# A joint inverse of two units by 16-row corners, with the middle block by matrix products, in a fused delta-rule attention and feed-forward kernel

## The chip, the cores and the metric

The kernel runs on one core of a Trainium2 chip. The metric is device time in microseconds (us) of one launch, as the median of several runs; before the change three runs gave a median of 634.74 us (633.33 to 635.35). The engines of the core are named PE (TensorE, matrix products; its weight load is listed as PEld), DVE (VectorE), ACT (ScalarE), POOL (GpSimd) and SP (SyncE, whose queue issues nearly all DMAs). Each engine takes its instructions in program order.

## The reference

Two layers follow each other, in float32: a linear attention with the delta rule over 4 batches, 8 heads, 768 tokens and head size 48, and a feed-forward layer with squared ReLU on 3072 tokens of width 384.

```
k_n = k / (norm(k) + 1e-6)
for t in range(S):
    y[t]  = q[t] @ state
    v_old = state^T @ k_n[t]
    state = state + beta[t] * outer(k_n[t], v[t] - v_old)
x   = y as (tokens, heads * 48)
out = relu(x @ w_in) ** 2 @ w_out          # w_in 384 x 2048, w_out 2048 x 384
```

## The kernel before

**Units.** The sequence is cut into 12 units of 64 tokens (`C`), each for all 4 batches and 8 heads, which gives 32 blocks of 64 by 64. In such a block the recurrence becomes the inverse of a lower triangle, built from beta and the products of the keys. The block is inverted by 32-row halves (`HB`): the two diagonal blocks of 32 rows by elimination on DVE, the block between them by two matrix products (`whole`). `solved` multiplies V by the inverse T, `onward` moves the state on and gives the attention's output `y`, and `moe` runs the feed-forward layer on a unit's 256 tokens. From unit 1 on, a list of places (`weave`) mixes the parts of one unit's attention into the matrix products of another unit's `moe`.

**The start.** Units 0 and 1 are treated together ahead of that. `load` and `normalize` fetch and normalize the keys, `static` forms the products of keys with keys and then of queries with keys, and sends the 32-row blocks through DRAM (`to_blocks`, L375) into one tile `lt` with 128 rows (L382), a row of which is one of the 32-by-32 triangles of units 0 and 1. `invert` with `both` set then inverts all 128 at once: 31 steps of two DVE instructions each (L453 multiplies a column by a row, L456 subtracts), between two scalings by beta (L446, L458). L464 transposes the result into `dd`. From `dd`, DMAs carry the diagonal blocks to their places in the T tiles `tt0` and `tt1` (L479) and a copy for the product with the upper block to `t1t` (L475), which L517 transposes for unit 0. L510 and L522 are the two products of `whole`, L512 and L528 the copies that follow them.

**The weights.** All 28 pieces of the feed-forward weights stay on chip, each split into a high and a low part. A piece goes through five stations: `fetch` (L126, DMA), `scaled` (L140, ACT), `words` (L148, L150, L152, DVE, into staging tiles `a` or `r` and `rest` or `h_l`), `high` (L158, ACT) and `low` (L165, L166 on PE, L167 on ACT). The staging tiles `a` and `r` have two buffers each, so the words of the third piece of a kind need the low of the first to have read them. Twenty pieces are split ahead of the first `moe` step, eight of them ahead of the inverse; the calls of `early` set how many stand between the parts of unit 0's chain. Before a low is issued, up to three highs may stand ready (`LAG`).

**The order.** The tail of the function, from L725, writes the order out by hand with `take`, `fetch`, `scaled`, `worded`, `highs`, `lows` and `early`; there is no scheduler behind it. What is written first is issued first on each engine's queue. The framework keeps eight DMA lanes for SP's queue: an issue waits until the one eight places ahead has landed.

The lines that set the start's order from the query products of units 0 and 1 on, with unit 2's keys loaded behind them:

```
for d in pair:
    take(d, 3)
    scaled(2)
ds_.append(load(2))                 # keys of unit 2
fetch(1)
scaled(4)
inverse, third = invert(ds_[0]), normalize(ds_[2])
take(inverse, HB - 1)
take(third, 1)
scaled(3)
```

Of the kernel before, what the change touches and what calls it, by code (L numbers as in the profile page):

```python
# [21 lines left out]
def kernel(  # L22
# [27 lines left out]
    HB = 32  # L50
    NC = 2
# [373 lines left out]

    def invert(d):


        both = d["u"] == 0
        lt, bt = ds_[1 if both else d["u"]]["lt"], d["bt"]  # L430
        nz = 1 if both else 2
        J = HB // nz
        if both:

            z = ttile[1].rearrange("p c h t -> p (c h t)").rearrange("p (j t) -> p j t", t=HB)
        else:
            z = apool.tile([P, J, HB], F32, name="z", bufs=1)
# [6 lines left out]
        room = mpool.tile([P, size], F32, name="h_h", bufs=3) if both else apool.tile([P, size], F32, name="tmp", bufs=1)  # L444
        if both:
            nc.vector.tensor_tensor(out=lt, in0=lt, in1=bt.unsqueeze(2).broadcast_to([P, HB, HB]), op=ALU.mult)  # L446
        for s in range(HB - 1):
# [4 lines left out]
            if both:  # L452
                nc.vector.tensor_tensor(out=tmp, op=ALU.mult, **factors)  # L453
            else:
                nc.vector.scalar_tensor_tensor(out=tmp, scalar=bt[:, s:s + 1], op0=ALU.mult, op1=ALU.mult, **factors)  # L455
# [4 lines left out]
        if both:  # L460


            dd = apool.tile([P, HB, HB], F32, name="lt", bufs=1)
            nc.vector.transpose(out=dd.rearrange("p r t -> p t r"), in_=z.rearrange("p j t -> p t j"))  # L464
            ds_[0]["low"] = dd[:, :H2]
            for x in range(2):
                part = dd[:, x * H2:(x + 1) * H2]
                if x:
                    nc.gpsimd.memset(ttile[1][:, :, :, :HB], 0.0)
                    yield  # L470
                t1t = apool.tile([P, H, HB], F32, name="t1t", bufs=1)
                ds_[x]["t1t"] = t1t
                for n in range(4):
                    up = n // 2 * C
                    nc.sync.dma_start(out=t1t[n * HB:(n + 1) * HB], in_=part[up:up + HB, n % 2::2])  # L475
                rows = ttile[x].rearrange("p c h t -> p (c h) t")
                for n in range(4):
                    q = slice(n * HB, (n + 1) * HB)
                    nc.sync.dma_start(out=rows[q, :, halves_of[n]], in_=part[q])  # L479
            return  # L480
# [13 lines left out]
    def whole(d):  # L494
# [5 lines left out]

        t1 = apool.tile([P, H, HB], F32, name="t1", bufs=1)
        if u:
            nc.vector.transpose(out=t1, in_=d["t1t"])
# [3 lines left out]
        for h in range(H2):  # L507
            c, e = h // H, h % H
            for b in range(2):
                nc.tensor.matmul(ps[at[h % 2][b], h // 2], lhsT=ap[lower[b], c, e, 0, :HB],  # L510
                                 rhs=tt[lower[b], c, e, HB:] if u else d["low"][lower[b], h], start=True, stop=True)
        nc.scalar.copy(out=m, in_=ps)  # L512
        if u:
            keys_on_state(d)
        yield
        if not u:
            nc.vector.transpose(out=t1, in_=d["t1t"])  # L517
# [5 lines left out]
        if u:  # L523
            queries_on_state(d)
# [186 lines left out]
    EARLY = (3, 4, 3)  # L711
# [12 lines left out]
    with tc.manual_schedule(engines=engines):  # L724
# [55 lines left out]
        chain = state_part(ds_[0])  # L780
        take(chain, 1)
        take(third, 1)
        worded(1)
        take(third, 1)
        highs(1)
        worded(1)
        for n, _ in zip(EARLY, chain):
            take(third)
# [63 lines left out]
```

## Time and profile before

| what | value |
|---|---|
| median of three runs | 634.74 us (633.33 to 635.35) |
| the profiled execution | 633.26 us |
| its span in the trace | 631.5 us |
| PE busy | 584.2 us (93%) |
| DVE busy | 412.3 us (65%) |
| ACT busy | 316.0 us (50%) |
| POOL busy | 30.2 us (5%) |

Cut at the joint inverse and at the end of the start, the stretches of the trace give, from the view of windows: from 0 to 30 us PE is busy for 16.8 of 30 us, DVE for 18.1; from 30 to 58.2, PE 9.2 of 28.2, DVE 25.8, ACT 12.7; from 58.2 to 88.2, PE 23.4 of 30, DVE 26.2, ACT 18.6; from 88.2 to 110, PE 18.1 of 21.8; from 110 to the end, PE 516.7 of 521.5. So the start is the part in which PE is not full.

How to read the rows that follow: a row of a timeline has its start, its length, the engine, the line of the program, the operation, output and inputs, the shape, the count and, in brackets, how long the engine sat idle and what ended it. A row of windows has the stretch, its length, the busy time of PE, PEld, DVE, ACT and POOL with counts, the clock granted to PE (1.00 is full), the mean busy share of the DMA engines, and GB/s. The chain of waits is followed back from the last instruction to what released it. Lines are those of the kernel before; L510 there is line 510.

### The profile page before, as it was taken

What the parts mean: (1) busy time and instruction counts of PE and PEld (TensorE: products, weight loads), DVE (VectorE), ACT (ScalarE), POOL (GpSimd) and SP (SyncE); (2) the same over time, 40 slices, a digit from 0 to 9 for tenths busy, and PEclk for the clock granted to TensorE, in tenths of its full rate; (3) what the DMA queues carried; (4) which work ended last, traced back from release to release, by engine and by line L of the source; (5) the groups of instructions that cost most, each with busy time, mean ns of one, the idle gap of its engine ahead of it and who ended that gap; (6) DMA issues with size and microseconds to landing.
All of it is one profiled execution on the core that took longest, in us unless ns stands there. A gap on an engine that the chain in (4) does not pass through costs nothing.

```text
span 631.5 us, 22895 instructions
## 1 busy us (share of the span) xinstructions
PE 584.2 (93%) x9904; PEld 550.1 (87%) x9904; DVE 412.3 (65%) x1126; ACT 316.0 (50%) x620; POOL 30.2 (5%) x53
## 2 busy tenths in 40 slices
PE   2940888999999999999999999999999999999997
PEld 1530567999999999999999999999999999999996
DVE  4799886685784784784774875875866856831211
ACT  4834678454445445535536445444554544355442
POOL 5001000001001001001001010010010010000000
PEclk9965899899999999999999999999999999999999
DMA  7784846214515417217227226236235143030101
GB/s 221 199 227 110 211 132 120 34 28 83 83 34 95 76 29 124 51 34 116 55 39 118 57 41 111 53 48 99 53 55 92 28 85 61 3 69 3 26 0 26
DMA packets 173548, 49.38 MB, mean 78 GB/s; under 512 B 165376, under 2 KB 168456, under 8 KB 173448
## 3 DMA queue, kind: packets, MB, share of 16 engines
q1 hardware_dynamic: 170984, 47.32, 38.0%
q8 instruction: 78, 1.28, 0.9%
q10 hardware_dynamic: 2336, 0.59, 0.5%
q14 instruction: 22, 0.18, 0.1%
q0 software_dynamic: 128, 0.01, 0.0%
HBM read 36.54 MB, written 10.49 MB: 74 GB/s over the span
## 4 chain that ended last, share of the span: by engine, by line
PE 84%; DVE 6%; ACT 4%; DMA 2%; SPq 2%; issue 1%; DVEq 0%; ACTq 0%
PE o L634 34%; PE h L647 32%; PE x L547 2%; PE g L547 2%; PE x L357 2%; PE x L571 2%; DVE tt L456 2%; DVE h_h L453 2%; PE x L587 2%; PE g L596 2%; PE g L357 1%; PE x L522 1%; PE h L510 1%; PE o L165 1%; PE h L613 1%
## 5 line engine op out<-in xcount | busy, mean ns | idle before, releaser
L634 PE MATMUL o<-w,h_h 128*128 128x384 f32 x768 | 204.2, 347 | 0.0
L654 ACT ACTIVATE r<-h 128x512 f32<-128x512 f32 x96 | 57.5, 599 | 230.2 <-PE h L647 230.1
L626 DVE TENSOR_TENSOR h_l<-r,h_h 128x512 fp32r<-128x512 f32 x96 | 67.3, 701 | 160.3 <-ACT h_h L657 160.3
L647 PE MATMUL h<-x_h,w 128*128 128x256 f32 x1152 | 169.0, 282 | 0.0
L647 PEld LDWEIGHTS h<-x_h,w 128*128 128x128 f32 x1152 | 154.6, 189 | 0.8
L634 PEld LDWEIGHTS o<-w,h_h 128*128 128x128 f32 x768 | 134.4, 189 | 3.2
L634 PE MATMUL o<-w,h_l 128*128 128x384 f32 x384 | 130.2, 339 | 0.0
L455 DVE SCALAR_TENSOR_TENSOR tmp<-lt,bt,z 128x126 f32<-128x126 f32 (+22 forms) x310 | 95.6, 308 | 7.5
L647 PE MATMUL h<-x_l,w 128*128 128x256 f32 x576 | 99.5, 281 | 0.0
L456 DVE TENSOR_TENSOR z<-z,tmp 128x126 f32<-128x126 f32 (+22 forms) x310 | 79.2, 256 | 10.6
L647 PEld LDWEIGHTS h<-x_l,w 128*128 128x128 f32 x576 | 81.6, 189 | 0.0
L634 PEld LDWEIGHTS o<-w,h_l 128*128 128x128 f32 x384 | 72.5, 189 | 0.0
L655 ACT ACTIVATE r<-r 128x512 f32<-128x512 f32 x96 | 60.7, 632 | 3.1
L657 ACT CAST h_h<-r 128x512 fp32r<-128x512 f32 x96 | 59.5, 620 | 3.0
L439 POOL MEMSET z<- 128x512 f32 x10 | 5.3, 528 | 435.2 <-DMA inv<-z 435.2
L357 PE MATMUL x<-kq 48*64 48x64 f32 (+1 forms) x608 | 20.4, 255 | 1.4 <-ACT kq L344 1.3
L357 PEld LDWEIGHTS x<-kq 48*64 48x64 f32 x608 | 17.9, 152 | 3.4 <-ACT kq L344 2.1
L341 PE MATMUL x<-plus,kpad 64*128 64x64 f32 x104 | 7.8, 246 | 11.8 <-DVE kpad L305 11.8
L528 ACT ACTIVATE tt<-x 32x256 f32<-32x256 f32 x44 | 16.4, 374 | 3.0 <-PE h L522 2.5
L367 DVE TENSOR_TENSOR ap<-x,mask 128x512 f32<-128x512 f32 x20 | 12.9, 686 | 7.5 <-PE x L357 7.5
L341 PEld LDWEIGHTS x<-plus,kpad 64*128 64x128 f32 x104 | 6.2, 157 | 12.0 <-issue 12.0
L442 POOL TENSOR_SCALAR_AFFINE_SELECT z<-z 64x512 f32<-64x512 f32 x20 | 16.0, 798 | 1.4
(125 smaller groups left out, 651.1 us busy)
## 6 DMA issues: line engine op xcount, KB each, us to landing
w<-in_moe_w_in_dram SPq DMA_DIRECT2D x12, 512.0 KB
w<-in_moe_w_out_dram SPq DMA_DIRECT2D x16, 384.0 KB
lt<-blocks SPq DMA_DIRECT2D x20, 256.0 KB
vt<-in_v_dram SPq DMA_DIRECT2D x48, 96.0 KB
out_dram<-a SPq DMA_DIRECT2D x46, 96.0 KB
kpad<-in_k_dram SPq DMA_DIRECT2D x88, 48.0 KB
qpad<-in_q_dram SPq DMA_DIRECT2D x88, 48.0 KB
blocks<-ap SPq DMA_DIRECT2D x40, 64.0 KB
```

The costliest lines, as they stand in the source:

```text
L357: nc.tensor.matmul(ps[j][to * C:(to + 1) * C, p, (x - first) * C:(x - first + m) * C], lhsT=kq[rows, c, p, b, 0], rhs=kq[rows, c, p, b, x: ...
L442: nc.gpsimd.affine_select(out=half, in_=half, pattern=[[nz, J], [-1, HB]], base=g, channel_multiplier=0, compare_op=ALU.not_equal, fill=1.0)
L455: nc.vector.scalar_tensor_tensor(out=tmp, scalar=bt[:, s:s + 1], op0=ALU.mult, op1=ALU.mult, **factors)
L456: nc.vector.tensor_tensor(out=z[:, :nj, s + 1:], in0=z[:, :nj, s + 1:], in1=tmp, op=ALU.subtract)
L528: nc.scalar.mul(out=right[upper[b], j, :, HB:], in_=ps[j][upper[b]], mul=-1.0)
L547: nc.tensor.matmul(dst[j][to, c, p], lhsT=d["kq"][rows, c, p, b, x], rhs=state[rows, b, c, p], start=(c == 0 and p == 0) if x else True, s ...
L626: nc.vector.tensor_tensor(out=h_l, in0=r, in1=h_h.bitcast(F32), op=ALU.subtract)
L634: nc.tensor.matmul(o[i], lhsT=a[:, e, i * P:(i + 1) * P], rhs=halves["wo", ft][w], start=(ft == 0 and n == 0), stop=(ft == FT - 1 and n == 2))
L647: nc.tensor.matmul(hp[:, e], lhsT=halves["wi", (kt, ft // EACH)][w][:, f], rhs=x[:, kt], start=(n == 0), stop=(n == 3 * KT - 1))
L654: nc.scalar.activation(out=r, in_=hp, func=AF.Relu)
L655: nc.scalar.activation(out=r, in_=r, func=AF.Square)
L657: nc.scalar.copy(out=h_h, in_=r)
```

## The change

The joint inverse gets a function of its own, `invert_both`, and `invert` keeps the later units. Each 32-by-32 triangle is now cut into two corners of 16 rows (`QB`), which are inverted side by side in 15 steps (L447 and L449 of the kernel after) on an access pattern that takes both corners at once. The result is transposed as before (L455), each unit's half of it is transposed once more (L460), and the 16-by-16 block between the corners comes from two sets of 64 small matrix products per unit: L469, a copy on ACT (L471), L477, and a subtraction on DVE (L478). The corners' products sit in four groups of 32 rows, one bank for each unit. The T block that unit 0's `whole` needs is now made by a transpose on chip (L481) instead of a DMA and a transpose; `whole` for unit 0 has a branch of its own (L546, L549, L554, L556). The keys of unit 2, the third unit, are loaded behind unit 0's T rows, and the values of unit 0 (V) take their place ahead of them; the normalization of unit 2 and the weight stations are placed anew.

```
+    def invert_both():
+        lt, bt = ds_[1]["lt"], ds_[0]["bt"].rearrange("p (g t) -> p g t", g=2)
...
+        def corners(x):
+            x = x[:, :QB, :QB]
+            return bass.AP(x.tensor, x.offset, [x.ap[0], (QB * HB + QB, 2), *x.ap[1:]])
...
+        nc.vector.tensor_tensor(out=ld, in0=ld, in1=bt.unsqueeze(3).broadcast_to(full), op=ALU.mult)
+        for s in range(QB - 1):
+            nj, nt = s + 1, QB - 1 - s
+            tmp = room[:, :2 * nj * nt].rearrange("p (g j t) -> p g j t", g=2, t=nt)
+            nc.vector.tensor_tensor(out=tmp, in0=ld[:, :, s:s + 1, s + 1:].broadcast_to([P, 2, nj, nt]),
+                                    in1=zd[:, :, :nj, s:s + 1].broadcast_to([P, 2, nj, nt]), op=ALU.mult)
+            nc.vector.tensor_tensor(out=zd[:, :, :nj, s + 1:], in0=zd[:, :, :nj, s + 1:], in1=tmp, op=ALU.subtract)
+            yield
+        nc.vector.tensor_tensor(out=zd, in0=zd, in1=bt.unsqueeze(2).broadcast_to(full), op=ALU.mult)
+        dd = apool.tile([P, HB, HB], F32, name="lt", bufs=1)
+        nc.vector.transpose(out=dd.rearrange("p r t -> p t r"), in_=z.rearrange("p j t -> p t j"))
+        parts = [dd[:, x * H2:(x + 1) * H2] for x in range(2)]
...
+        for part, dt in zip(parts, turned):
+            nc.vector.transpose(out=dt, in_=part)
...
+        for x in range(2):
+            ps, places = quarters()
+            for h, n, q in places:
+                nc.tensor.matmul(ps[q, h], lhsT=ds_[x]["ap"][q, h // H, h % H, 0, n % 2 * HB:(n % 2 + 1) * HB],
+                                 rhs=parts[x][q, h, QB:], start=True, stop=True)
+            nc.scalar.copy(out=mids[x], in_=ps)
+        yield
+        for x in range(2):
+            ps, places = quarters()
+            for h, n, q in places:
+                low = slice(n * HB, n * HB + QB)
+                nc.tensor.matmul(ps[q, h], lhsT=turned[x][low, h], rhs=mids[x][low, h], start=True, stop=True)
+            nc.vector.tensor_tensor(out=parts[x][:, :, QB:], in0=parts[x][:, :, QB:], in1=ps, op=ALU.subtract)
+            if x == 0:
+                ds_[0]["t1"] = mpool.tile([P, H2, HB], F32, name="h_h", bufs=3)
+                nc.vector.transpose(out=ds_[0]["t1"], in_=parts[0])
...
-    EARLY = (3, 4, 3)
+    EARLY = (3, 3, 3)
...
-        ds_.append(load(2))
+        load_v(ds_[0])
         fetch(1)
         scaled(4)
-        inverse, third = invert(ds_[0]), normalize(ds_[2])
-        take(inverse, HB - 1)
-        take(third, 1)
+        inverse = invert_both()
+        take(inverse, QB - 1)
         scaled(3)
         take(inverse, 1)
-        load_v(ds_[0])
-        fetch(5)
+        worded(2)
+        take(inverse, 1)
+        highs(2)
+        chain = state_part(ds_[0])
+        take(chain, 1)
+        worded(1)
+        fetch(2)
+        ds_.append(load(2))
+        third = normalize(ds_[2])
+        take(inverse, 1)
+        fetch(3)
         load_q(ds_[2])
...
```

On ACT, behind the scaling of the weights for the start: what stood there before (`w` are weight pieces, `y` the squares of unit 2's keys, `m` the copy between the two products of `whole`, `tt_108` unit 0's T tile).

```order
L140 ACTIVATE w_448<-w_448 128x512
L289 ACTIVATE y<-kpad_104 128x384 x2
L140 ACTIVATE w_450<-w_450 128x512
L140 ACTIVATE w_452<-w_452 128x384
L140 ACTIVATE w_598<-w_598 128x384
L512 COPY m<-h 128x256
L295 ACTIVATE s_673<-n_672 128x16
L158 CAST w_790<-a 128x512
L528 ACTIVATE tt_108<-x 32x8x32 x2
```

The same place after (`t_645` and `t1t` hold the middle products of units 0 and 1, `x_l` is the copy between the two products of `whole`).

```order
L141 ACTIVATE w_448<-w_448 128x512
L141 ACTIVATE w_450<-w_450 128x512
L141 ACTIVATE w_452<-w_452 128x384
L141 ACTIVATE w_595<-w_595 128x384
L471 COPY t_645<-x 128x256
L471 COPY t1t<-h 128x256
L159 CAST w_863<-a 128x512
L159 CAST w_865<-r 128x512
L549 COPY x_l<-h 32x512 x2
L159 CAST w_1029<-a 128x384
L556 ACTIVATE tt_108<-x 32x16x32 x2
```

The squares of unit 2's keys have left this place; the copies of the middle products stand directly behind the scaling of the nineteenth weight piece (w_598 before, w_595 after).

On DVE, behind the joint inverse's transpose: the rows after, up to the mask of unit 0's query scores (`lt` is `dd`, `h_h` and `z` the two transposed halves, then `h_h` the T block).

```order
L455 STREAM_TRANSPOSE lt<-tt_110 128x32x32
L460 STREAM_TRANSPOSE h_h<-lt 128x512
L460 STREAM_TRANSPOSE z<-lt 128x512
L149 TENSOR_SCALAR a<-w_418 128x512
L151 TENSOR_SCALAR w_418<-w_418 128x512
L153 SCALAR_TENSOR_TENSOR rest<-w_418 128x512
L149 TENSOR_SCALAR r<-w_420 128x512
L151 TENSOR_SCALAR w_420<-w_420 128x512
L153 SCALAR_TENSOR_TENSOR h_l<-w_420 128x512
L478 TENSOR_TENSOR lt<-lt,h 128x16x16
L481 STREAM_TRANSPOSE h_h<-lt 128x512
```

Before, behind the same transpose (L464) stood the sums of unit 2's squares, the words of w_418 and w_420, the transpose of `t1t` and the rest of unit 2's normalization. The normalization now stands behind the words of nine pieces, and two instructions that wait for PE and ACT (L478, and a second L478 behind the words of the next piece) are new.

On SP, behind the eighteenth weight piece: before, and then after.

```order
L126 DMA w_452<-in_moe_w_out_dram 128x768
L252 DMA kpad_104<-in_k_dram 64x4x48 x8
L126 DMA w_598<-in_moe_w_out_dram 128x768
L475 DMA t1t<-lt 32x8x32 x4
L479 DMA tt_108<-lt 32x16x32 x4
L246 DMA vt<-in_v_dram 64x8x48 x4
L126 DMA w_700<-in_moe_w_out_dram 128x768
```

```order
L127 DMA w_452<-in_moe_w_out_dram 128x768
L247 DMA vt<-in_v_dram 64x8x48 x4
L127 DMA w_595<-in_moe_w_out_dram 128x768
L493 DMA tt_108<-lt 32x16x32 x4
L127 DMA w_908<-in_moe_w_out_dram 128x768
L127 DMA w_910<-in_moe_w_out_dram 128x768
L253 DMA kpad_104<-in_k_dram 64x4x48 x8
```

V has moved ahead of the wait for the inverse, the keys of unit 2 behind it, and the T block's four DMAs for unit 0 are gone.

More of the change, by code (lines that the diff above doesn't have):

```diff
@@ L50 @@
     HB = 32
+    QB = HB // 2
     NC = 2
@@ L443, in invert @@
                                     channel_multiplier=0, compare_op=ALU.not_equal, fill=1.0)
-        room = mpool.tile([P, size], F32, name="h_h", bufs=3) if both else apool.tile([P, size], F32, name="tmp", bufs=1)
-        if both:
-            nc.vector.tensor_tensor(out=lt, in0=lt, in1=bt.unsqueeze(2).broadcast_to([P, HB, HB]), op=ALU.mult)
+        room = apool.tile([P, size], F32, name="tmp", bufs=1)
         for s in range(HB - 1):
@@ L459, in invert @@
         halves_of = [slice(n % 2 * HB, (n % 2 + 1) * HB) for n in range(4)]
[L460 to L480, printed above, removed]
         inv = dram.tile([4, H2, HB, HB], F32, name="inv")
@@ L499, in whole @@
         lower = [slice(b * C + HB, (b + 1) * C) for b in range(2)]
+        if not u:
+            low, t1 = d["low"], d["t1"]
+            m = mpool.tile([P, H2, HB], F32, name="x_l", bufs=1)
+            ps = ps_h.tile([P, PC], F32, name="h").rearrange("p (h t) -> p h t", h=H2)
+            for h in range(H2):
+                for b in range(2):
+                    nc.tensor.matmul(ps[upper[b], h], lhsT=ap[lower[b], h // H, h % H, 0, :HB], rhs=low[lower[b], h],
+                                     start=True, stop=True)
+            for b in range(2):
+                nc.scalar.copy(out=m[upper[b]], in_=ps[upper[b]])
+            yield
+            ps = x_tile(u).rearrange("p (h t) -> p h t", h=H2)
+            for h in range(H2):
+                for b in range(2):
+                    nc.tensor.matmul(ps[upper[b], h], lhsT=t1[upper[b], h], rhs=m[upper[b], h], start=True, stop=True)
+            for b in range(2):
+                nc.scalar.mul(out=tt.rearrange("p c h t -> p (c h) t")[upper[b], :, HB:], in_=ps[upper[b]], mul=-1.0)
+            yield
+            return
         t1 = apool.tile([P, H, HB], F32, name="t1", bufs=1)
-        if u:
-            nc.vector.transpose(out=t1, in_=d["t1t"])
+        nc.vector.transpose(out=t1, in_=d["t1t"])
         m = apool.tile([P, H, HB], F32, name="m", bufs=1)
@@ L510, in whole @@
                 nc.tensor.matmul(ps[at[h % 2][b], h // 2], lhsT=ap[lower[b], c, e, 0, :HB],
-                                 rhs=tt[lower[b], c, e, HB:] if u else d["low"][lower[b], h], start=True, stop=True)
+                                 rhs=tt[lower[b], c, e, HB:], start=True, stop=True)
         nc.scalar.copy(out=m, in_=ps)
-        if u:
-            keys_on_state(d)
+        keys_on_state(d)
         yield
-        if not u:
-            nc.vector.transpose(out=t1, in_=d["t1t"])
         ps = [x_tile(u)[:, :H * HB].rearrange("p (k t) -> p k t", k=H) for _ in range(2)]
@@ L779 @@
         load_v(ds_[1])
-        chain = state_part(ds_[0])
+        highs(1)
         take(chain, 1)
+        early(EARLY[0])
+        take(pair[0])
+        take(chain, 1)
+        early(1)
         take(third, 1)
[L783 to L788, printed above, removed]
-            early(n)
-            take(pair[0])
+        early(EARLY[1] - 1)
+        take(third)
+        take(chain, 1)
+        early(EARLY[2])
         scaled(2)
```

43 lines of the change are left out of this document (30 added, 13 removed).

## The prediction

> **What bounds the kernel now.** I read the page first, then the chain of waits over the first 130 us, then the timelines of VectorE (DVE), TensorE (PE), ScalarE (ACT) and the DMA queue (SPq) there.
>
> ```profile
> span 631.5 us, 22895 instructions
> PE   2940888999999999999999999999999999999997
> by line: DVE tt L456 8.4%; DVE h_h L453 8.4%; PE h L647 6.2%; issue 6.2%; PE o L165 5.1%; PE o L634 5.1%; ACT w L140 3.7%; ACT w L158 3.4%; ACT w L167 3.4%; DMA w<-in_moe_w_in_dram 3.0%; DVE w L150 2.5%; DMA kpad<-in_k_dram 2.4%; DMA vt<-in
> ```
>
> PE is full from about 110 us on: its row of slices is 9 throughout. Nothing in the change touches that part, so whatever it does must happen ahead of it, where the slices fall to 0 and 4, and a gain ahead shifts the rest as a whole. The chain of waits says who holds the start up: L456 and L453, the two instructions of each step of the joint inverse, are 8.4% each of the first 130 us.
>
> ```profile
> 30.16 1.23 DVE L446 TENSOR_TENSOR lt<-lt,bt 128x1024 f32<-128x1024 f32 x1
> 31.49 0.19 DVE L453 TENSOR_TENSOR h_h<-lt,tt 128x31 f32<-128x31 f32 x1
> 31.95 0.22 DVE L453 TENSOR_TENSOR h_h<-lt,tt 128x60 f32<-128x60 f32 x1
> 33.03 0.27 DVE L453 TENSOR_TENSOR h_h<-lt,tt 128x112 f32<-128x112 f32 x1
> 56.15 1.97 DVE L464 STREAM_TRANSPOSE lt<-tt 128x1024 f32<-128x1024 f32 x1
> ...
> 46.88 0.32 PE L357 MATMUL x<-kq 48*64 48x64 f32 x2
> 58.26 1.07 PE L510 MATMUL h<-lt,ap 32*32 32x32 f32 x64 [11.06 <-DVE lt L464]
> L510 PE MATMUL h<-lt,ap x64: 228/236/255, 58.3 to 59.1; 32*32 32x32 f32 x64
> ```
>
> DVE starts the joint inverse at 30.16 and its last transpose (L464) ends at 58.12. PE finishes the query scores at 47.20 and then waits 11.06 us for that transpose. That is the stretch the change shortens.
>
> **Step 1, the inverse on DVE.** Before: 31 steps, 31.49 to 54.88, plus two scalings and the transpose. After: 15 steps, each over two corners at once, with 30, 56, 78, 96, 110, 120, 126, 128 elements and then back down. A step of two instructions takes 0.46 us at 31 elements (31.49 to 31.95) and twice 0.27 plus two gaps of 0.035 at 112, so 0.61; on that line the 15 steps sum to 8.6 us against 23.4. The two scalings fall from 1024 to 512 elements, 1.23 to about 0.7 each (estimate: half the elements plus the fixed part that the 31-element row shows). The big transpose stays 1.97. So the inverse ends at 30.16 + 0.75 + 8.6 + 0.7 + 1.97 = 42.2, 15.9 us earlier. Two transposes of 512 elements (L460) are new.
>
> ```profile
> 62.83 0.44 DVE L517 STREAM_TRANSPOSE t<-t1t 128x256 f32<-128x256 f32 x1
> 66.75 0.35 DVE L148 TENSOR_SCALAR r<-w 128x384 int32<-128x384 int32 x1
> 68.01 0.35 DVE L148 TENSOR_SCALAR a<-w 128x384 int32<-128x384 int32 x1
> 73.00 0.42 DVE L148 TENSOR_SCALAR a<-w 128x512 int32<-128x512 int32 x1
> 74.53 0.42 DVE L148 TENSOR_SCALAR r<-w 128x512 int32<-128x512 int32 x1
> ```
>
> 256 elements take 0.44 and 1024 take 1.97, so 0.95 each: 44.1. Behind them stand the words of two 512-wide weights, 1.53 us each (73.00 to 74.53; a 384-wide one is 1.26, 66.75 to 68.01): 47.2. Then DVE has nothing to do until PE returns the first middle block, so strided corners that cost some tens of per cent more are free: the cover is the idle time up to 54.7 found below. If that cover were gone, each extra us counts in full.
>
> **Step 2, where the 15.9 us stop.** The new products (L469) stand on PE behind the query scores, which end at 47.20 because unit 1's queries come late; nothing there changes. 128 products at the pace of L510 (64 in 1.07 us) end at 49.4. The copy that hands them on (L471) stands on ACT behind nine weight scalings:
>
> ```profile
> 47.75 2.95 ACT L140 ACTIVATE w<-w 128x384 f32<-128x384 f32 x6
> 43.93 7.63 SPq L252 DMA_DIRECT2D kpad<-in_k_dram  x8
> 46.77 1.28 SPq L252 DMA_DIRECT2D kpad<-in_k_dram  x2
> ...
> 46.00:48.00 2.00, 1.19 (x46) 1.00 (x38) 1.86 (x5) 1.43 (x5) 0.00 (x0) 0.50 1.04 399
> 52.00:54.00 2.00, 0.00 (x0) 0.00 (x0) 1.77 (x7) 0.96 (x3) 0.00 (x0) 0.50 0.66 155
> 54.00:56.00 2.00, 0.00 (x0) 0.00 (x0) 1.86 (x5) 1.45 (x3) 0.00 (x0) 0.50 0.17 68
> ```
>
> Six of the nine end at 50.70, two more at their pace (0.5) at 51.75. The ninth needs the nineteenth weight, which is issued behind the four V loads, as it was behind eight key loads before. Before, the eighth of those ended at 51.56, and the DMA share fell from 1.04 (46 to 48) to 0.17 between 54 and 56. After, the same bytes are queued with half the issues, and the fifth place in the queue falls at about 46.8 (where the fifth key load starts) instead of 51.6. So it lands no later than about 54.5 and perhaps without any wait; I take 52.6, since the low DMA share of the window 52 to 54 shows a gap that early issue closes. Scaling 0.5, copy 0.4: the first middle block is on chip at **53.5** (bounds 52.2 and 55.4).
>
> **Step 3, PE, ACT and DVE in turn.** From 53.5: L477 of the first half 1.1 (as L510) to 54.7; DVE subtracts 256 elements, 0.45, to 55.2, and transposes 512 for the T block, 0.95, to 56.2; PE's L546 1.07, to 56.4, ACT's two copies 1.1, to 57.6; PE meanwhile L477 of the second half, to 57.5, DVE's subtraction to 58.0; L554, 0.9, to 58.6. The T DMA of unit 0 starts at 55.3 on SP, 3 us before L475's 58.14, and four DMAs of T1 (2.67 us of SP's time) are gone. V was late before:
>
> ```profile
> 66.76 3.09 DMA vt<-in_v_dram
> 58.14 2.67 SPq L475 DMA_DIRECT2D t1t<-lt  x4
> 63.98 3.41 SPq L246 DMA_DIRECT2D vt<-in_v_dram  x4
> ```
>
> Its last load came in at 69.85 and unit 0's solve (L571) waited for it. After, V is in long before, and the T rows, issued 55.3 to 57.9, land by some 61.0 with the same 3.09 us. The solve stands behind three weight lows at about 63, so neither is late.
>
> **Step 4, the weights on DVE and PE.** From 58.0 DVE has ten words left, the mask, the normalization of unit 2 (which stood earlier before) and the state. The third and fourth word need staging buffers that the lows of the first two weights read:
>
> ```profile
> 64.42 2.08 PE L165 MATMUL o<-a,plus 128*128 128x512 f32 x2
> 66.72 0.63 PE L166 MATMUL o<-rest,plus 128*128 128x512 f32 x1
> 70.50 1.12 PE L165 MATMUL o<-r,plus 128*128 128x512 f32 x2
> ...
> 64.00:66.00 2.00, 2.00 (x41) 1.19 (x30) 1.81 (x6) 1.41 (x4) 0.00 (x0) 0.50 0.64 107
> 68.00:70.00 2.00, 0.94 (x40) 0.73 (x41) 1.93 (x5) 1.10 (x2) 0.00 (x0) 1.00 0.88 196
> ```
>
> The first low took 64.42 to 67.35, 2.93 us, at granted clock 0.50; the next, at 1.00, about 1.4 (70.50 to 71.9). After, PE has been at work since 53.6 with short gaps, so I take the mean, 2.25, for the first: 58.6 to 60.9. Word three starts at 60.2 (0.9 lost), word four at 62.05 (0.6 lost) and ends at 63.3. Then:
>
> ```profile
> 57.98 0.99 DVE L293 TENSOR_REDUCE n<-y 128x8 f32<-128x384 f32 x2
> 63.19 0.13 DVE L297 TENSOR_SCALAR s<-s 128x16 f32<-128x16 f32 x1
> 64.61 0.96 DVE L305 TENSOR_TENSOR kpad<-kpad,s 128x768 f32<-128x768 f32 x1
> 69.27 1.22 DVE L407 TENSOR_TENSOR ap<-ap,mask 128x1024 f32<-128x1024 f32 x1
> 77.60 0.55 DVE L590 TENSOR_TENSOR state<-state,x 128x384 f32<-128x384 f32 x1
> ```
>
> Mask 1.15, three wide words 4.6, sums of squares 0.95, ScalarE's root 0.35, 1.42 and 0.9 for the rest of the normalization, state 0.93, three words 3.8: together 14.1 us without a gap, to 77.4. ACT's own work from 53.5 to there is some 16 us, PE's less, so DVE sets the pace. Unit 2's keys are issued at about 59 to 65 (SP: T some 2.6 like T1, two weights 0.9, eight loads 5 to 7.63) and are needed by ACT at about 66: a bound of 1 us, which I count as nothing because the words in front of their sums last to 69.
>
> **Step 5, to the common point.**
>
> ```profile
> 81.26 0.50 ACT L158 CAST w<-a 128x384 fp32r<-128x384 f32 x1
> 82.14 1.23 ACT L140 ACTIVATE w<-w 128x512 f32<-128x512 f32 x2
> 83.26 0.86 ACT L616 CAST x_h<-h 128x384 fp32r<-128x384 f32 x2
> 88.16 1.08 ACT L344 COPY kq<-x 128x512 f32<-128x512 f32 x2
> ...
> 87.27 0.46 PE L341 MATMUL x<-plus,kpad 64*128 64x64 f32 x8
> ```
>
> After the last word ACT does a high and a low (0.9, from 81.26 to 82.14) and two scalings (1.12, to 83.26), then x_h: 79.45, against 83.26 before. One low fewer follows (three, not four). The last needs the bank that ACT frees at 80.65, PE takes 1.07, and the transposes of unit 2 and the copy L344 follow 0.9 later: 82.65. The same copy starts at 88.16 before. From there on both programs have the same instructions in the same order. **Gain 5.5 us.** In one line: the inverse ends 15.9 earlier; of that DVE gives back 1.9 for the added L460, 7.5 in idle time (47.2 to 54.7), 1.4 for the subtractions and the transpose of step 3 less L517's 0.44, and 1.5 in buffer waits; 3.6 are left, and 1.9 come from one low fewer ahead of the copy and from waits that DVE has between 58 and 84 now and would not have.
>
> The profiled execution took 633.26 us, 1.76 around its span; less 5.5 is 627.8. The median of the three runs is 634.74, 1.5 above, so I predict **629.2** for the median.
>
> [...] The window from 64 to 66 shows clock 0.50 and that from 68 to 70 shows 1.00, after PE had been busy from 63.41. [...] But the window from 46 to 48, in which PE still works off the scores (1.19 of 2 us), stands at 0.50 too; hence my mean.
>
> L510 puts 64 products of two row groups into one bank within 1.07 us. [...]
>
> **The rivals.** First: PE's clock is full before the first low, and the nineteenth weight doesn't make ACT wait. Both buffer waits go (1.5) and step 2 gains 1.3, perhaps more where four row groups run denser than two: 7 to 9 us, 626 to 628. For it: PE works from 53.6. Against: the gaps in step 3, and the 0.50 from 46 to 48.
>
> Second: the gain is there, but SP or the small products take part of it. SP starts the T rows 2.9 us earlier and no longer issues T1 (2.67) and V (3.41) there, but eight key loads (5 to 7.63), so what it issues next comes 1.4 to 4 us earlier, less than 5.5; four row groups at twice L510's price cost three sets on the path 3.2 us. 630.7 to 632.7. Against: what SP issues next is first read in step 5 or later, 10 us on.
>
> Third: it is absorbed, because the stage after the common point is paced by something that doesn't move. 632.8 to 636.6. Against: the chain there runs through ACT, DVE and PE in turn, all of which shift.
>
> Fourth, slower: ACT stands at the nineteenth weight, with the only copy that lets PE and DVE go on behind it. Each us that it lands past 52.6 costs one. It decides from a landing at 58.1; at 60.5 the kernel is at about 637. Before, all of these bytes were in by 56, which speaks against it.
>
> Fifth, slower by far: products of four row groups take turns on one bank. Then a set of 64 lasts 64 times the 236 ns of one of L510's, 15 us, and four new sets add over 40 us to the path: some 680. Against: L510's 64 products of two row groups share one bank and start 17 ns apart.
>
> **How the numbers follow.** Forecast, 628 to 630.5: 0.45. First rival 0.25, second 0.12, third 0.11, slower 0.07 (0.05 by the weight, the fourth; 0.02 by the bank, the fifth). A measurement of this kernel tells about 0.3% from no change, 1.9 us: faster 0.82, same 0.11, slower 0.07. The range reaches from the low end of the first rival to just inside the absorbed case: 625.6 to 633.6.
>
> **What would show it.** DVE: the big transpose ends near 42.2, then idle time from about 47 to 54.7 that ends with PE. ACT: the ninth scaling ends near 53.1, and x_h starts near 79.5. PE: no wait for V; L477 about 1.1 us a set; granted clock 0.50 when the first low starts. The copy at 88.16 moves to about 82.7. Wrong it would be if ACT's ninth scaling came past 56, if L469 and L477 took several us each, or if the shift at that copy weren't found in the total.

## The result, and the profile after

The kernel before took 634.04 us (median of four runs, 633.29 to 635.35) on this chip, the changed one 643.63 us (four runs, 641.84 to 645.41): ratio 1.0149, 95% interval 1.0114 to 1.0184. It is slower by some 9.6 us where the prediction had 5.5 us less, and it lies outside the range. The profiled execution of the changed kernel took 641.84 us with a span of 640.1.

I read DVE first, because the change is made there. This is its timeline; its lines are those of the changed kernel.

```profile
40.63 2.05 DVE L455 STREAM_TRANSPOSE lt<-tt 128x1024 f32<-128x1024 f32 x1
46.35 0.69 DVE L153 SCALAR_TENSOR_TENSOR h_l<-w 128x512 fp32r<-128x512 uint32 x1
59.81 0.42 DVE L478 TENSOR_TENSOR lt<-lt,h 128x256 f32<-128x256 f32 x1 [12.76 <-PE h L477]
...
65.08 0.42 DVE L478 TENSOR_TENSOR lt<-lt,x 128x256 f32<-128x256 f32 x1 [2.87 <-PE x L477]
...
71.19 0.36 DVE L149 TENSOR_SCALAR a<-w 128x384 int32<-128x384 int32 x1 [3.60 <-PE o L166]
...
91.23 1.02 DVE L670 TENSOR_TENSOR x_l<-h,x_h 128x384 fp32r<-128x384 f32 x2 [2.54 <-ACT x_h L669]
...
98.88 1.28 DVE L368 TENSOR_TENSOR ap<-x,mask 128x512 f32<-128x512 f32 x2
```

The inverse is as early as forecast: the large transpose ends at 42.7 (42.2 forecast), the words behind it at 47.0 (47.2). Then DVE stands still until 59.81 instead of 54.7, waits again for the second half (L478 at 65.08) and for the buffer of the third of the ten words that are left (71.19). x_l (L670) starts at 91.23; before it was 83.77. What ended DVE's long wait is PE's L477, so PE is next.

```profile
47.20 1.78 PE L469 MATMUL x<-lt,ap 32*32 32x16 f32 x114
52.34 0.35 PE L469 MATMUL x<-lt,ap 32*32 32x16 f32 x12 [3.37 <-issue]
...
52.54 1.70 PE L469 MATMUL h<-lt,ap 32*32 32x16 f32 x112
55.80 0.40 PE L469 MATMUL h<-lt,ap 32*32 32x16 f32 x13 [1.55 <-issue]
...
55.99 1.77 PE L477 MATMUL h<-t,h_h 16*32 16x16 f32 x113
59.35 0.40 PE L477 MATMUL h<-t,h_h 16*32 16x16 f32 x14 [1.58 <-issue]
60.38 1.76 PE L546 MATMUL h<-lt,ap 32*32 32x32 f32 x58 [0.62 <-DVE lt L478]
...
63.76 1.21 PE L477 MATMUL x<-t1t,z 16*32 16x16 f32 x76 [0.97 <-issue]
...
68.46 0.64 PE L554 MATMUL x<-x_l,h_h 32*32 32x32 f32 x15 [2.14 <-issue]
69.02 2.08 PE L166 MATMUL o<-a,plus 128*128 128x512 f32 x2
```

Two things stand here that the prediction did not have. A set of L469 or L477 is 128 rows, not 64: 114 + 14 for unit 0's L469. And five times PE sits idle and then goes on *in the middle of a run of independent products*, with nothing in the profile that it waited for ("issue"): 3.37, 1.55, 1.58, 0.97 and 2.14 us, 9.61 in all. They are evenly spaced in the program: behind the first pause come 12 rows, 4 single ones (left out here) and 112, 128 in all, and then the second pause; behind that 13, 2 single ones and 113, again 128, and then the third. The first low starts at 69.02; 58.6 was forecast, and before it was 64.42.

What comes every 128 rows? The page counts what each engine ran, and each DMA queue's packets. Of the kernel before, these two rows (engines; then the queue that carries instructions):

```profile
PE 584.2 (93%) x9904; PEld 550.1 (87%) x9904; DVE 412.3 (65%) x1126; ACT 316.0 (50%) x620; POOL 30.2 (5%) x53
q8 instruction: 78, 1.28, 0.9%
```

and of the changed one:

```profile
PE 594.3 (93%) x10416; PEld 559.6 (87%) x10416; DVE 400.9 (63%) x1098; ACT 317.2 (50%) x621; POOL 29.0 (5%) x53
q8 instruction: 82, 1.34, 0.9%
```

512 more rows of matrix products, each with a weight load of its own (PEld), and 4 more packets of some 16 KB (1.28 MB in 78) on the instruction queue: one packet for 128 pairs of weight load and product, which is why I read this queue as the one that feeds PE. In the stretch from 46 to 69 us the view of DMAs has, for the kernel before and then for the one after:

```profile
q8 instruction: 2, 0.03, 0.7%
```

```profile
q8 instruction: 5, 0.08, 1.7%
```

Two packets before, five after, and after the change a pause behind each of the five. Cut into windows of 0.1 us, the view books them at 49.7, 53.5, 57.0, 61.4 and 64.8; this is the first, and its 61.6% of 16 engines over 0.1 us make about 1.0 us of one engine.

```profile
q8 instruction: 1, 0.02, 61.6%
```

PE goes on at 52.34, 55.80, 59.35, 63.76 and 68.46, that is 2.3 to 2.6 us after four of them and 3.7 after the last; the next one is booked 1.0 to 2.1 us after PE has gone on. So the trace books one packet for every 128 pairs that PE runs, and I read a packet as one piece of PE's program. From the start of one piece to the start of the next it takes 3.5 us twice (52.34 to 55.80 to 59.35), and 4.4 and 4.7 after that. A piece of 128 of these small pairs runs in 1.9 us (1.91 for L477 in one piece, in the run with early lows below); for the rest PE is idle. The chain of waits that ended last leads through all five pauses.

On ACT the copy of the first middle block came late too, and farther on ACT waited for a word:

```profile
55.14 0.54 ACT L141 ACTIVATE w<-w 128x384 f32<-128x384 f32 x1 [2.63 <-DMA w<-in_moe_w_out_dram]
55.58 0.35 ACT L471 COPY t<-x 128x256 f32<-128x256 f32 x1
...
85.85 0.51 ACT L159 CAST w<-r 128x384 fp32r<-128x384 f32 x1 [3.62 <-DVE h_l L153]
...
90.74 0.83 ACT L669 CAST x_h<-h 128x384 fp32r<-128x384 f32 x2
...
94.09 1.08 ACT L345 COPY kq<-x 128x512 f32<-128x512 f32 x2
```

The scaling of the nineteenth weight (55.14) held the copy to 55.58, so that the first middle block was on chip at 55.9, past the forecast's bound of 55.4. The 3.62 us at 85.85 are DVE's normalization of unit 2 and the update of the state, which now stand between two words.

### The profile page after: what moved, and what is told of

Read it like the earlier page. It is cut to its first block, busy times and chain, and to the rows that moved or that the text cites. A ratio compares the mean times of both kernels' runs of the same rounds, so it can differ in the third digit from the quotient of the medians.

```text
span 640.1 us, 23893 instructions
## 1 busy us (share of the span) xinstructions
PE 594.3 (93%) x10416; PEld 559.6 (87%) x10416; DVE 400.9 (63%) x1098; ACT 317.2 (50%) x621; POOL 29.0 (5%) x53
## 3 DMA queue, kind: packets, MB, share of 16 engines
q8 instruction: 82, 1.34, 0.9%
## 4 chain that ended last, share of the span: by engine, by line
PE 85%; DMA 4%; SPq 3%; ACT 3%; issue 3%; DVE 2%; ACTq 0%; DVEq 0%
PE o L687 33%; PE h L700 31%; PE x L358 2%; PE x L600 2%; PE g L600 2%; DMA w<-in_moe_w_in_dram 2%; PE x L640 2%; PE x L624 2%; PE g L649 2%; PE g L358 1%; SPq L253 1%; PE x L576 1%; PE h L567 1%; PE h L666 1%; PE x L342 1%
## 5 line engine op out<-in xcount | busy, mean ns | idle before, releaser
L141 ACT ACTIVATE w<-w 128x384 f32<-128x384 f32 (+1 forms) x28 | 16.0, 612 | 3.3 <-DMA w<-in_moe_w_out_dram 3.3
```

## The experiments

Lines below the edits are numbered as in each variant's own program, so a line can differ by ten or twenty from that of the changed kernel. Each ratio is to the kernel before in the same rounds. Times of one variant scatter by up to 3 us around their median, so differences between two variants are taken from their ratios.

**Is it the position in PE's program?** 32 idle products (64 pairs) are put on PE behind unit 0's query scores, and nothing else is changed.

```
+            if d is pair[0]:
+                idle = ps_g.tile([P, 2, PC], F32, name="g")
+                for _ in range(32):
+                    nc.tensor.matmul(idle[:HB, 0, :HB], lhsT=ident[:HB, :HB], rhs=ident[:HB, :HB], ...)
```

> 32 idle products (64 pairs of weight load and matmul, into a bank nobody reads) are put on PE behind unit 0's query scores, where PE waits for a DMA anyway. Supply theory (PE's instructions come in pieces of 128 pairs, and dense small products use a piece up faster than the next arrives): every pause moves 64 pairs earlier, the first from pair 114 of L469 to about pair 50, later ones every 128 pairs; as many pauses, same total within 1.5 us (642 to 645). Rival (the pauses belong to the sets: a bank that changes, a change of shape): they stay at pair 114 of L469, 114 of L477.

642.99 us in one run. PE's timeline:

```profile
47.77 0.92 PE L469 MATMUL x<-lt,ap 32*32 32x16 f32 x50
49.65 1.20 PE L469 MATMUL x<-lt,ap 32*32 32x16 f32 x76 [0.96 <-issue]
...
56.12 1.26 PE L469 MATMUL h<-lt,ap 32*32 32x16 f32 x78 [4.57 <-issue]
57.48 0.92 PE L477 MATMUL h<-t,h_h 16*32 16x16 f32 x50
60.00 1.25 PE L477 MATMUL h<-t,h_h 16*32 16x16 f32 x78 [1.59 <-issue]
```

The pauses have moved by just the 64 pairs: the first comes behind 50 rows of L469 instead of 114, the third behind 50 rows of L477 instead of 113. They belong to places in the instruction stream, not to a line, a bank or an operand. The packets have moved with them: the view of DMAs books them at 47.3, 53.0, 57.2, 61.2 and 65.1, and PE goes on 2.3 to 3.1 us after each (49.65, 56.12, 60.00, and 63.70 and 67.43, which are not shown). Place and packet together are why "issue" is read here as waiting for the program.

**Is the price the number of instructions?** Half as many products in L469 and L477, each twice as wide: one head's block serves two heads, which changes the blocks between the corners for every second head. A set is then 64 pairs, the size that the prediction took.

```
-            return ps, [(h, n, ...) for h in range(H2) for n in range(4)]
+            return ps, [(h, n, ...) for h in range(0, H2, 2) for n in range(4)]
...
-                nc.tensor.matmul(ps[q, h], lhsT=..., rhs=parts[x][q, h, QB:], ...)
+                nc.tensor.matmul(ps[q, h:h + 2], lhsT=..., rhs=parts[x][q, h:h + 2, QB:], ...)
```

> The changed kernel with half as many small products in L469 and L477: one head's block serves a pair of heads, so that each product is 32 columns wide instead of 16 and a set is 64 pairs of instructions, the size that the prediction's sum took (the blocks between the corners are those of a neighbouring head for every second head: this part of the computation is changed). 256 pairs go, two pieces of the supply. If pairs and pieces are the price: two pauses of more than 1.5 us fewer, the first low starts at about 63 instead of 69.02, and with 0.88 us of total per us of first low (643.6 and 69.02 against 635.4 and 59.64 without products) the time is 637.5 to 639. Rival: the price of a set is its columns or its bank, not its instructions (twice the width at half the count takes as long): pauses as before, 642 to 645.

637.25 us, ratio 1.0054 (1.0033 to 1.0075): some 6 us of the 9.6 are gone. PE:

```profile
47.58 1.07 PE L469 MATMUL x<-lt,ap 32*32 32x32 f32 x64
53.00 0.43 PE L469 MATMUL h<-lt,ap 32*32 32x32 f32 x14 [3.62 <-issue]
...
57.08 1.07 PE L477 MATMUL h<-t,h_h 16*32 16x32 f32 x64 [3.65 <-ACT t L471]
```

A set takes 1.07 us, as in L510's row, and one pause is left of five; the first low starts at 63.81. (What L477 waits for at 57.08 is the copy behind the nineteenth weight, which lands later here than in the changed kernel.) The same columns with half the instructions cost far less, so the rival (columns, bank) falls.

**What do all products cost, and what is left without them?** L460, L469, L471, L477 and L478 are taken out, so the blocks between the corners stay zero; the order is that of the changed kernel. And, as a second run, the same with the old inverse of 31 steps.

```
-        for part, dt in zip(parts, turned): ...            # L460
-        for x in range(2): ...                             # L469, L471
-                nc.tensor.matmul(ps[q, h], lhsT=turned[x][low, h], ...)      # L477, and L478
```

> The changed kernel without L460, L469, L471, L477 and L478: the block between the corners is left as the corners' inverse leaves it, zero, so that block of T is left out; all else in the same order. Supply theory: the first low starts near 59 (behind the nineteenth weight, which ACT still waits for until 55.1, and L546, L549, L554), 10 us earlier than 69.0, and the kernel is at 632 to 635. Rival (weight theory: the wait of ACT for the nineteenth weight is what costs): that wait is still there, so 640 or above.

> The order of the changed kernel with the 31-step inverse of the kernel before: no corners, no products between them, no ACT copies and no subtractions; T block by a transpose on chip, V ahead, keys of unit 2 behind T as in the change. Supply theory: DVE's inverse ends near 58.4, the first low starts near 64, and the kernel is at 634 to 637. Rival (order theory: it is the moved V, keys and normalization that cost): it stays at 641 or above.

Without the products: 635.36 us, ratio 1.0014 (0.9996 to 1.0033). With 31 steps: 639.98, ratio 1.0086 (1.0059 to 1.0112). So the products cost 1.3% of 634, some 8.5 us, and the shorter inverse is worth 4.6 us against the long one in this order. But the shorter inverse without any products only equals the kernel before, and the old inverse in the new order (with unit 0's T block transposed on chip) is 5.5 us slower than the kernel before: the order by itself costs. With 31 steps, neither of the two expected ranges held. The timelines without the products (ACT, then PE, then DVE) show where the 16 us stop:

```profile
55.11 0.54 ACT L141 ACTIVATE w<-w 128x384 f32<-128x384 f32 x1 [2.03 <-DMA w<-in_moe_w_out_dram]
...
46.98 1.92 PE L527 MATMUL h<-lt,ap 32*32 32x32 f32 x64
57.20 0.31 PE L535 MATMUL x<-x_l,h_h 32*32 32x32 f32 x2 [8.31 <-ACT x_l L530]
...
61.81 0.36 DVE L149 TENSOR_SCALAR a<-w 128x384 int32<-128x384 int32 x1 [11.01 <-PE o L166]
```

The first low starts at 59.64 there (58.6 was forecast), because its place on PE is behind both products of `whole` (L527 and L535 here). The second of them waits 8.31 us for its copy, which stands on ACT behind the nineteenth weight (55.11) and two highs, and the third word waits 11.01 us for the buffer that the low reads.

**The banks of unit 1.** The new functions draw five banks where the old ones drew two, so later products of unit 1 that alternated between two banks all fall on one, and PE waits 0.79 (L576) and 0.44 us (L624) near 127 and 133 us. One more draw restores the alternation.

```
             ps = x_tile(u).rearrange("p (h t) -> p h t", h=H2)
+            turn[0] += 1
```

> One number in the bookkeeping is put right: invert_both and the new branch of whole draw five times from the rotation of PSUM banks where the kernel before drew twice, so unit 1's products meet other banks. Bank theory: unit 1's L554 to L640 alternate between x and h again, the waits of 0.8 us (L576) and 0.4 us (L624) on ACT go, and the kernel is 1.5 to 2 us faster than the changed one, about 642. Rival (these waits only follow from a shifted ACT): no change, 643.6.

642.84 us, ratio 1.0119 (1.0098 to 1.0141), against 1.0149 (1.0114 to 1.0184) without it. Both waits are gone from the list of PE's waits; the gain by the ratios, some 2 us, lies within the overlap of the two intervals.

**The normalization of unit 2, early again.** Its keys are fetched ahead of the T rows, and their sums and scaling stand in DVE's wait.

```
         fetch(1)
+        ds_.append(load(2))
+        third = normalize(ds_[2])
         scaled(4)
...
         worded(2)
+        take(third, 2)
```

> The changed kernel, with the keys of unit 2 fetched ahead of the T block's DMAs again, and their normalization on DVE in its waits at 57 to 70 us instead of between the ninth and tenth words. All products stay. If the late normalization holds up the split (ACT waits 3.62 us for the tenth word, PE 2.81 for ACT), both waits go and x_h starts some 3 us earlier than 90.74: 639.5 to 641.5. Rival: that stretch is paced by the lows on PE, or the early normalization delays the third word by as much: 643 to 645.

641.95 us, ratio 1.0110 (1.0083 to 1.0138), between the two. ACT's 3.62 us and PE's 2.81 us are gone, but ACT now waits 1.66 and 1.04 us for the keys ahead of the copy that `whole` needs, and the first low slips to 71.38: one wait bought with another.

**Unit 1's sets elsewhere.** They are not needed before unit 1's `whole`, so they are moved behind unit 0's solve (L477 behind the update of the state). A second run adds the early normalization and the banks.

```
-        take(inverse, 1)            # L477, L478 of unit 1 behind L546
...
         take(third, 1)
+        take(inverse, 1)            # L469 of unit 1
         early(EARLY[1] - 1)
         take(third)
         take(chain, 1)
+        take(inverse, 1)            # L477, L478 of unit 1
```

> The changed kernel, with unit 1's two sets of small products (and what hangs on them: one copy, one subtraction, eight DMAs) moved behind unit 0's solve, to where PE waits for ACT and DVE anyway; unit 0's sets stay where they were. If the sets and the pauses of PE's instruction supply set the pace from 47 to 69 us, 256 of the 640 pairs leave that stretch, with two of the five pauses: 2 x 1.8 + about 3.2 us; the first low starts at 62 to 63.5 instead of 69.02, and the time falls to 636 to 639. Rival: what the order of the rest costs (normalization late, waits for buffers) sets the pace whatever the products do: first low early, but 641 to 644.

> The two edits together (unit 1's sets late, unit 2's normalization early), and one more draw so that unit 1's products alternate between the two banks as before. If the causes are separate, 6 + 3 + 1 us go: 632 to 635, about the kernel before. If both edits shorten one and the same wait: 636 to 639.

642.49 us, ratio 1.0136 (1.0098 to 1.0175), and 642.49, ratio 1.0124 (1.0103 to 1.0144). The first lies in the range of its rival, the second in neither range. The first low starts at 63.07 in the first, as expected, and yet nothing is gained. PE of the first, then its DVE:

```profile
77.43 0.33 PE L649 MATMUL x<-vt,kpad 64*64 64x48 f32 x1 [2.12 <-issue]
...
82.25 1.08 PE L477 MATMUL x<-t1t,z 16*32 16x16 f32 x106 [1.20 <-issue]
```

```profile
83.39 0.42 DVE L478 TENSOR_TENSOR lt<-lt,x 128x256 f32<-128x256 f32 x1 [3.56 <-PE x L477]
```

The new place lies among the 64-pair sets of the solve and the state, and those have now become part of a dense run: one pause falls in L649, one in the moved L477, and DVE with all words behind L478 waits 3.56 us. In the second run that pause is 4.34 us. The dense run cost its pauses at the new place too.

**Large products between the small ones.** As the run before, with the highs of the first two words ahead of the last scalings on ACT, and one low (three large products) behind L469 and one behind L477 of unit 0.

```
         worded(2)
+        highs(2)
+        take(inverse, 1)            # L469 of unit 0
+        lows(1)
+        scaled(2)
...
+        take(inverse, 1)            # L477, L478 of unit 0
+        lows(1)
+        scaled(1)
```

> As the run before, and the highs of the first two words ahead of the last scalings on ACT, their lows on PE between unit 0's sets (one behind L469, one behind L477). The large products between the small ones give the supply time to fetch (a low of three products is 6 instructions in about 2.6 us), so the pauses behind them should shrink or go; the third and fourth words need not wait 3 to 11 us for their buffers. If so 628 to 632, faster than the kernel before. Rival: the lows delay unit 0's sets by their 5.4 us at half clock and the state comes that much later: 634 to 638.

638.75 us, ratio 1.0066 (1.0041 to 1.0090): better by 3.7 us, less than either range expected. PE:

```profile
52.09 0.40 PE L469 MATMUL x<-lt,ap 32*32 32x16 f32 x14 [3.28 <-issue]
...
55.28 1.91 PE L477 MATMUL h<-t,h_h 16*32 16x16 f32 x128
...
79.46 1.06 PE L477 MATMUL h<-t1t,z 16*32 16x16 f32 x105 [3.23 <-issue]
```

Behind a low (52.42 to 55.35, 2.93 us at granted clock 0.50) the whole set of L477 runs without a pause (128 rows in 1.91 us from 55.28), which I read as the supply catching up while PE works on large products. What is left behind that is unit 1's L469 with 0.39 us, its L477 with 3.23, and DVE's wait for it (4.51).

**Unit 1's sets among the expert products.** In a first run close behind the first hidden columns; in a second one farther back, with a group of at least nine large products ahead of each set, and with the third and fourth word of DVE moved into its waits as well (and unit 2's blocks fetched after the sets have been read).

```
-        take(inverse, 1)
...
+                parts.append((joint, [0.05, 0.12, 0.14]))      # second run: [0.2, 0.24, 0.26]
...
         scaled(2)
+        worded(1)                                              # second run
```

> The run e8_lows with unit 1's two sets taken out of the stretch ahead of x_h and put among the large products of the first expert stage, where PE is the bound and its instructions last 0.2 to 0.8 us each. If the supply is the mechanism, it keeps up there and the sets cost only their 256 pairs, 2.2 to 2.9 us of PE; DVE's wait of 4.51 us for L477 and ACT's of 6.21 us go, x_h starts near 84 instead of 88.03: 635 to 638 in all. Rival: the pauses follow the products wherever they stand: 638 to 641.

> As e10_weave, with three things moved: the third word on DVE ahead of unit 0's subtraction, into DVE's wait; the fourth word ahead of the sums of unit 2's squares (whose keys came 1.94 us late); and unit 1's two sets behind the whole of the second expert pair's large products instead of next to unit 2's 64-wide transposes and scores, where a crossing still cost 1.81 us. If DVE's waits were the bound, x_h starts at 80.5 to 82 instead of 83.65, and the sets, now between products of 0.2 us and more, cost their 256 pairs without a pause, 2.2 to 2.9 us: 632 to 635, at least level with the kernel before. Rival: the pauses follow the products there too, or the first stage is paced by something that the order does not touch: 636 to 639.

The first: 639.05 us, ratio 1.0068 (1.0045 to 1.0092), no better, and in the range of the rival. x_h starts at 83.65 as expected, but that place turned out to lie right in front of unit 2's scores, which are 64-wide products themselves; L469 and L477 paused 0.73 and 1.81 us, and DVE's masks behind them started at 97.64 instead of 96.18. The second: 634.47 us, ratio 0.9985 (0.9971 to 0.9999), level with the kernel before or faster by a hair, and the best with the products in. Its PE:

```profile
52.26 0.40 PE L469 MATMUL x<-lt,ap 32*32 32x16 f32 x14 [3.10 <-issue]
52.60 2.08 PE L166 MATMUL o<-a,plus 128*128 128x512 f32 x2
...
55.45 1.91 PE L477 MATMUL h<-t,h_h 16*32 16x16 f32 x128
...
93.52 1.26 PE L469 MATMUL x<-lt,ap 32*32 32x16 f32 x128
...
98.14 0.68 PE L477 MATMUL h<-t1t,z 16*32 16x16 f32 x59 [0.94 <-issue]
```

4.04 us of pauses instead of 9.61, and x_h at 81.97. A pause stays even here (0.94), so "no pause among large products" did not come true to the letter: eleven rows of large products stood between the two small sets, and this pause was left.

**What can the earlier inverse be worth?** The same order without L460, L469, L471, L477 and L478 (blocks between the corners zero).

> The order of e12_best without L460, L469, L471, L477 and L478: the blocks between the corners stay zero, so that part of the computation is left out. It bounds what the earlier inverse can be worth: if the order takes up the 16 us as far as the data allow, 628 to 631, and the difference from e12_best (3 to 5 us) is what the products cost when they are placed well. Rival: with all products gone the time is still at or above 633, and no order turns the earlier inverse into time.

631.05 us, ratio 0.9930 (0.9911 to 0.9949): 4.5 us faster than before. No run puts the long inverse into this order, so how much of the 4.5 is the inverse and how much the order stays open. Against the run without products in the changed kernel's own order (1.0014), the order alone is worth 0.84%, 5.3 us. Against the run with the products (0.9985) the products still cost 0.55%, 3.5 us, in their best place.

## Why the prediction was wrong

**Step 1 was right.** The transposes, the 15 steps and the words of two weights ended within 0.5 us of their forecast; L460 took 0.71 and 0.67 us, less than the 0.95 taken.

**Steps 2 and 3 failed first in the size of a set.** The step said "128 products at the pace of L510 (64 in 1.07 us)" and "L477 of the first half 1.1 (as L510)". L510's row has x64, and I read it as 64 products. The code makes 32 (16 heads, two halves); each shows as two rows. A set of 64 products is therefore 128 rows and takes 1.8 to 1.9 us at granted clock 0.50 (1.44 at 1.00, at 71.19 in the first run with unit 1's sets moved; 1.26 at 93.52 in the last run with products); with half the products it took the 1.07 us that the step had. Counting the products of L510 in the code beside the count in its row would have shown the factor.

**Step 3 also mis-sized unit 0's own two products.** It priced L546 at 1.07 us and L554 at 0.9, from L510 and L522. They have the same 64 rows each, and the same clock of 0.50, but the run without the small sets, where nothing else disturbs them, has 1.92 us for the first (L527 there) and as much for the second. In the code L510 writes to four groups of 32 output partitions in turn, the new branch to two; no run varied that alone.

**The same steps lacked a cost that the trace of before hardly shows.** From 46 to 69 us the kernel before ran two pieces of PE's program, one while PE waited (booked at 49.5) and one beside large products (65.0); the change puts 640 pairs, five pieces, into a stretch with little else for PE, and PE paused at each. No rival had it. The first low missed its forecast by 10.4 us. Of these, 2.4 lie ahead of the first middle block (on chip at 55.9, not 53.5), where the first two pauses (3.37 and 1.55) and the nineteenth weight coincide; 4.7 are the other three pauses (1.58, 0.97, 2.14); the remaining 3.3 are L477, L546 and L554, longer than priced. Without the small products the first low missed by 1.0 us.

**Step 2's nineteenth weight** could be scaled from 55.1 on; 52.6 was taken. In the changed kernel the copy behind it ended at 55.93, and PE went from unit 1's L469 to L477 at 55.99 without a wait: the weight or the two pauses alone would have held L477 to that moment. Without the products the weight alone holds up PE, by the 8.31 us shown above. The fourth rival, ACT standing there beyond 58.1, did not happen.

**Step 4 was mis-sized in two terms.** The first low took 69.02 to 71.90, 2.88 us instead of the 2.25 taken as a mean (2.93 and 1.4 give 2.17): granted clock was 0.53 there (0.50 up to 71) and 1.00 only from 72 on. I had counted on steady work of PE for the clock. The pauses are not what kept it low: without products, with half of them, and with unit 1's sets moved, no such pause stood in the 10 us ahead of the first low (59.64, 63.81, 63.07), and it took the same 2.9 us at 0.50. In the last run with products PE worked from 52.30 to 62.00 without a gap, and the clock (third number from the end) stayed at 0.50:

```profile
52.30:62.00 9.70, 9.70 (x214) 6.19 (x213) 3.31 (x7) 3.85 (x8) 0.00 (x0) 0.50 0.51 100
```

It rose there between 68 and 69. In the kernel before it had risen between 67 and 68, behind 3.94 us of work without a gap (63.41 to 67.35); here 9.7 us did not bring it. So the length of the work alone does not give the clock in these runs; the first rival, which had it full before the first low, falls, and what does bring it stays open. The second term is unit 2's keys, counted as nothing. That holds for the keys, not for the normalization that comes with them: it holds up ACT's tenth high (3.62 us) and PE's low (2.81). Without products x_h came at 82.70, 3.2 us later than the forecast's 79.45, and in the last order without products at 80.36.

**Step 5's common point was the wrong row.** From L344 on the step gave "the same instructions in the same order". From that copy to the end the kernel before takes 543.3 us, the changed one 546.0 (640.1 less 94.09). DVE, which the step left out, paces this place; its first mask of unit 2 before was

```profile
91.95 1.28 DVE L367 TENSOR_TENSOR ap<-x,mask 128x512 f32<-128x512 f32 x2
```

3.79 us behind the copy, and at 98.88 after (the last row of DVE's first fence above), 4.79 behind it; from the mask to the end it is 539.6 and 541.2. Of the other 1.7 us, up to 1.2 are the two waits of unit 1 on one bank (0.79 and 0.44), which the one added draw removes. The instructions were the same, their banks were not.

**The rivals.** The second named the small products, at 3.2 us and as a doubled row time of four row groups; it had a factor of two right for another reason and far too little. The fifth, turns on a bank, is refuted: 114 rows of four row groups in one bank ran in 1.78 us, under 16 ns each. No run shows such turns.

**Two causes, not one.** The forecast was 5.5 us less and the result 9.6 us more. The sign went wrong by the products, which cost 8.5 us. But in this order the gain was absorbed as well: without the products the time is that of the kernel before (1.0014), in the range of the third rival, because the order takes back (5.5 us) what the shorter inverse gives (4.6). The late normalization, the copy's place behind the nineteenth weight and the longer L546 and L554 are all part of it; no run tells how the 5.5 us divide among them. With the products taken out and the order mended the kernel is 4.5 us faster, and that this lies near the 5.5 forecast is luck: it is another order, and the products are missing.

What stays open: why a packet takes between 1.0 and 2.9 us to be booked after PE enters a piece. In the stretch of the first pause the DMA engines' mean share was 1.06 (48 to 50) and 1.31 (50 to 52), later 0.02 and 0.04 (54 to 58), which fits a queue behind data loads. The longest pause, 4.57 us in the run with idle products, fits it too: its packet was booked at 53.0, 3.4 us after PE entered the piece, at shares of 1.34 and 1.31. No run changed the loads to test it. How many pieces the supply can hold ahead was not measured either.

## What to carry to other kernels

Price many small matrix products by their instructions, not by their columns: count the rows that the trace shows for one product, and lay the run out in pieces of 128 pairs, each of which took 3.5 us and more here where its pairs alone take 1.9, and ran without a pause behind 2.93 us of large products. Rows alone are not the whole price: 64 of them took 1.07 us in L510 and 1.92 in the branch that replaced it. An "issue" pause that recurred every 128 pairs, with a packet on the instruction queue each time, pointed here to the supply of the program. And a shared point from which "all is the same" has to be checked on every engine that feeds it, banks included.

## What the runs showed of the hardware

- The instruction queue carried 78 packets (1.28 MB) beside 9904 pairs of weight load and product before the change, and 82 (1.34 MB) beside 10416 after: some 16 KB for 128 pairs. In the dense run of small products one piece took 3.5 us (52.34 to 55.80 to 59.35); 128 such pairs without a pause took 1.91.
- Behind three large products between two sets, 2.93 us at granted clock 0.50, 128 small pairs ran without a pause, in 1.91 us (the run with early lows, from 55.28).
- A float32 product of 32 by 32 by 16 stands in the trace as two rows (64 products of L469, 128 rows); 114 rows over four row groups in one bank took 1.78 us.
- 64 rows of 32 by 32 by 32 products, at granted clock 0.50, took 1.07 us where the code writes to four groups of 32 output partitions in turn (L510) and 1.92 where it writes to two (L527 without products).
- PE was busy without a gap for 9.7 us (52.30 to 62.00 in the last run with products) at granted clock 0.50; the clock rose between 68 and 69.
